# Attention with a mixture of experts on one core: six weight buffers, the first copies on ScalarE, later means, two steps run in the lead-in

## The chip, the cores and the metric

The kernel runs on one core of a Trainium2 chip. The metric is the device time of one execution in microseconds. Three runs of the kernel before gave a median of 1029.19 us (1027.43 to 1030.52). Five engines work side by side, each in the order of its own queue: TensorE (PE, matmuls and transposes), VectorE (DVE), ScalarE (ACT), GpSimd (POOL) and SyncE (SP), which here only issues DMAs.

## The reference

Four batches, eight heads, 576 positions, 64 features. Causal attention is mixed by a gate with a memory term, and the result goes through four experts whose outputs are summed with weights. All is fp32.

```python
scores = scale * np.matmul(q, k.transpose(0, 1, 3, 2))
scores = np.where(causal, -1000000000.0, scores)
a = np.exp(scores - scores.max(-1, keepdims=True))
a /= a.sum(-1, keepdims=True) + 1e-09
local = np.matmul(a, v)
q_p = phi(q)                       # elu(q) + 1
mem_out = einsum('bhsd,bhde->bhse', q_p, M_prev) / (einsum('bhsd,bhd->bhs', q_p, z_prev) + 1e-06)
x = g * mem_out + (1 - g) * local  # then [2304, 512]
p = domain_probs / (domain_probs.sum(-1, keepdims=True) + 1e-09)
for e in range(4):
    h = np.maximum(x @ w1[e], 0.0)       # [2304, 1024]
    out += p[:, e:e + 1] * (h @ w2[e])   # [2304, 512]
```

## The kernel before

Matmul operands are split into a high part (rounded) and a low part (what is left), and products are summed as high x high, high x low and low x high. So xh and xl, hh and hl, w1h and w1l, w2h and w2l, kha, khb and kl all are such parts.

The expert work runs in 40 phases. A phase is one half of one expert (four tiles of 128 hidden features, HF = 4) for one or two groups of 256 tokens: in phases 0 to 4 and 37 to 39 one group, between them two. In a phase the first layer makes h for the four tiles (`mm1`: matmuls L790, then hh on ScalarE L799 and hl on VectorE L800), then the second layer makes y (`mm2`: matmuls L820, accumulation on VectorE L834 and L836).

Each phase needs eight raw weight tiles of 256 KB. `w_dma` asks for a tile on SyncE's queue into a buffer of the tag stg; `w_prep` splits a tile (the high part on ScalarE, L205, or on GpSimd, L207; the low part mostly on GpSimd, L209) and then asks for the tile four further on. There were four buffers, so that tile went into the buffer just split.

The attention runs as 28 tasks of two heads each (12 of them joint, with the first 256 positions; 16 with the other 320) after a lead-in (`first_run`) that does the first 256 positions of batch 0 in an order written out by hand (the string ORDER; each word is a step). A task is cut into steps: load q, k, v (`t_load`), the feature map phi (ex on ScalarE, qp on VectorE L288, rl on GpSimd L292, rn on VectorE L300 to L310), transposes of q and k (`t_trq`, `t_trk`: tiles tq and tk), the split of v (`t_v`, L399 and L400), scores (`j_qk`, `s_qk`), exponentials, normalization, transposes of the probabilities (pt), the output (`j_o`, `s_o`). Scores are one matmul over 128 rows that hold the high part twice, so half of kha, khb and qz is copied to the other 64 partitions by DMAs from SBUF to SBUF (`dup_k` L352; the qz copies L371 and L376). Task i uses the set of buffers i % 2.

The memory matrices of a batch (mr) are split on GpSimd into ms (`batch_prep`, L231 and L232) once for each of the seven runs of four tasks; the output matmuls read ms.

Every step has a slot number and a priority within it. Sorted, they make one list, and a planner hands them out between the parts of the expert work, paced by estimated costs: a step is emitted when the share of attention done has fallen behind the share of expert work done (`target`). In the lead-in, words w1 and w3 also run the steps up to slots -9 and -8. What is emitted is each engine's order; nothing is reordered later.

Of the kernel before, what the change touches and what calls it, by code (L numbers as in the profile page):

```python
# [8 lines left out]
F32 = mybir.dt.float32  # L9
F32R = mybir.dt.float32r  # L10
# [39 lines left out]
def tile_attention_moe(  # L50
# [51 lines left out]
    sp = ctx.enter_context(tc.tile_pool(name="sp", bufs=2))  # L102
# [5 lines left out]
    def f(ap):  # L108
        return ap.bitcast(F32)
# [18 lines left out]
    for i in range(2):  # L128
        o, d = i * 13 * P, {}
# [39 lines left out]
    NSTG = 4  # L169
    wpos = {"dma": 0, "prep": 0}  # L170
    stg = {}

    def w_dma():
        j = wpos["dma"]
        if j >= len(wseq):
            return
        wpos["dma"] += 1
        i, kind, fc = wseq[j]
        e, hf = halves[i]
        f0 = (hf * HF + fc) * P  # L180
        t = sp.tile([P, DM], F32, tag="stg", name=f"stg{j}", bufs=NSTG)
        stg[j] = t
        if kind == "1":
            nc.sync.dma_start(
                out=t.rearrange("p (c f) -> p c f", c=NKD),
                in_=w1[e, :, f0 : f0 + P].rearrange("(c p) f -> p c f", p=P),
            )
        else:
            nc.sync.dma_start(out=t, in_=w2[e, f0 : f0 + P, :])
# [35 lines left out]

    def batch_prep(r):
        zb, mr, _ = bdat[r]
        ms = sp.tile([P, NPAIR, 4, D], F32R, tag="ms", name=f"ms{r[0]}_{r[1][0]}", bufs=2)
        m4 = mr.rearrange("p (a j) d -> p a j d", j=2)
        hi = ms[:, :, 0:4:3]  # L230
        nc.gpsimd.tensor_scalar(hi, m4, 1.0, 1.0, ALU.mult, ALU.mult)  # L231
        nc.gpsimd.tensor_tensor(ms[:, :, 1:3], m4, f(hi), ALU.subtract)  # L232
        bdat[r][2] = ms
# [7 lines left out]
    for b, cs in RUNS[1:]:  # L241
        for a in range(NPAIR):
            t = Task()
# [88 lines left out]
    def split_q(pt, qa, qb, n, scale):  # L332
        nc.scalar.activation(qa[A, 0:n], pt[A, 0:n], AF.Copy, scale=scale)
        nc.scalar.activation(qb[Bh, 0:n], pt[Bh, 0:n], AF.Copy, scale=scale)
        nc.vector.scalar_tensor_tensor(
            qa[Bh, 0:n], pt[A, 0:n], scale, f(qa[A, 0:n]), ALU.mult, ALU.subtract
        )
        nc.vector.scalar_tensor_tensor(
            qb[A, 0:n], pt[Bh, 0:n], scale, f(qb[Bh, 0:n]), ALU.mult, ALU.subtract
        )  # L340

    def split_k(pt, qk, c0, n):
        o = slice(c0, c0 + n)
        for x, k_ in ((A, qk["kha"]), (Bh, qk["khb"])):
            nc.scalar.activation(k_[x, o], pt[x, 0:n], AF.Copy)
        for x, k_ in ((A, qk["kha"]), (Bh, qk["khb"])):
            nc.vector.tensor_tensor(qk["kl"][x, o], pt[x, 0:n], f(k_[x, o]), ALU.subtract)

    def dup_k(qk, c0, n):
        o = slice(c0, c0 + n)  # L350
        for x, y, k_ in ((A, Bh, qk["kha"]), (Bh, A, qk["khb"])):
            nc.sync.dma_start(out=f(k_[y, o]), in_=f(k_[x, o]))  # L352

    def flat(ap):
        return ap.rearrange("p j d -> p (j d)")

    def t_trq(t):
        pt = to_tile(f"tq{t.i}")
        qk, last = t.qk, t.nk == NCH
        w = len(t.cs) * P  # L360
        for i in range(len(t.cs)):

            tr(pt[:, i * P : (i + 1) * P], flat(t.nat["q"][:, i]), P)
        if last:
            tr(pt[:, w : w + P], flat(t.nat["k"][:, 4]), P)
        split_q(pt, qk["qa"], qk["qb"], w, SCALE)
        if last:
            split_k(pt[:, w:], qk, 4 * P, D)
            dup_k(qk, 4 * P, D)
        for h, (x, q_) in enumerate(((A, qk["qa"]), (Bh, qk["qb"]))):  # L370
            nc.sync.dma_start(  # L371
                out=f(qk["qz"][x, h * GW : (h + 1) * GW]), in_=f(q_[x, 0:GW])
            )
            if last:
                o = 2 * GW + h * D
                nc.sync.dma_start(out=f(qk["qz"][x, o : o + D]), in_=f(q_[x, w - D : w]))  # L376

    def t_trk(t):
        pt = to_tile(f"tk{t.i}")
        m = min(t.nk, NCH - 1)  # L380
        for c in range(m):
            tr(pt[:, c * P : (c + 1) * P], flat(t.nat["k"][:, c]), P)
        split_k(pt, t.qk, 0, m * P)
        dup_k(t.qk, 0, m * P)

    def t_trqp(t):
        pt = to_tile(f"tp{t.i}")
# [296 lines left out]
    def ev(slot, prio, fn, cost=0.0):  # L684
        events.setdefault(slot, []).append((prio, len(events.get(slot, [])), fn, cost))

    seen = set()
    for t in tasks:
        s0 = t.s0
        ld = -9 + t.i if t.i < 2 else s0 - 7  # L690
        PQ = PR
        if t.run not in seen:
            seen.add(t.run)
            ev(s0 - (9 if t.i else 8), 9, lambda r=t.run: batch_load(r))
            ev(s0 + 1, 9, lambda r=t.run: batch_prep(r))
            if t.cs == CB and t.b == 0:
                for i in range(2):
                    ev(s0 - 12, 9, lambda i=i: zeros(i))
        ev(ld, 6.3 if t.cs == CA else 8, lambda t=t: t_load(t))
        ev(s0 + PQ["phi1"][0], PQ["phi1"][1], lambda t=t: t_phi1(t))  # L700
        ev(s0 + PQ["phi2"][0], PQ["phi2"][1], lambda t=t: t_phi2(t))
        ev(s0 + PQ["phi3"][0], PQ["phi3"][1], lambda t=t: t_phi3(t))
        if t.joint:
            ev(s0 - 3, 20, lambda t=t: t_phi4(t))
        ev(s0 + PQ["trq"][0], PQ["trq"][1], lambda t=t: t_trq(t), 109.0 * len(t.cs))
        ev(s0 + PQ["trk"][0], PQ["trk"][1], lambda t=t: t_trk(t), 109.0 * t.nk)
        ev(s0, PQ["v"], lambda t=t: t_v(t))
# [27 lines left out]
    steps = []  # L735
# [135 lines left out]
    def first_run():  # L871
# [201 lines left out]
        def f_w(j):  # L1073
            w_prep(0, "1" if j < HF else "2", True)
            if j in (1, 3):
                while si[0] < len(steps) and steps[si[0]][0] <= (-9 if j == 1 else -8):
                    run_step()

        def f_d(j):
            z_ = moe_bank(f"id{j}")  # L1080
            for _ in range(2):
                nc.tensor.matmul(z_, lhsT=hh[0][:, 0:P], rhs=hh[0], start=True, stop=True)
# [6 lines left out]
        rc4 sc5 nm20 pt2 rn0 sc7 m1 mk50 nm30 nm31 m0 sc6 mk51 pe2 pt3 nm40 nm41  # L1089
        ex50 ex51 tq0 w1 mk70 pe3 mk71 w2 rc5 eq0 tq1 eq1 w3 ex70 pt4 mk60 ou0 w4 d9  # L1090
        ex71 nm51 tq3 mk61 xh0 nm50 rc7 xl0 eq3 d2 ex61 nm71 pt5 ex60 rc6 nm70 pe4
        nm60 nm61 pe5 tq2 ou1 pt7 w5 eq2 pt6 pe7 xh1 ou2 xl1 pe6 w6 ou3 xh2 xl2 xh3
        xl3 w7 d12
        """
        calls = {k[2:]: g for k, g in locals().items() if k.startswith("f_")}

# [7 lines left out]
        for _ in range(NSTG):  # L1104
            w_dma()
        m4 = M_prev[b].rearrange("(a j) d e -> j d a e", j=2)
        for j in range(2):
            o = slice(j * D, (j + 1) * D)
# [10 lines left out]
        for word in ORDER.split():  # L1119
            name = word.rstrip("0123456789")  # L1120
# [8 lines left out]
        out=mask[:, 4 * P :],  # L1129
        in_=mask[:, 4 * P :],  # L1130
# [104 lines left out]
```

## Time and profile before

| | us |
|---|---|
| median of three runs | 1029.19 |
| profiled execution | 1027.72 |
| its span, first to last instruction | 1025.9 |
| busy in the span: TensorE | 1005.7 (98%) |
| VectorE | 671.5 (65%) |
| GpSimd | 581.4 (57%) |
| ScalarE | 487.3 (47%) |
| DMA queue of SyncE, share of 16 engines | 43.9% |

A busy time counts matmuls that may overlap at their ends, so a busy TensorE is not always TensorE at its peak. An idle time in brackets stands before an instruction, with what ended it. Names are the program's without buffer numbers; L and a number is a line of the kernel.

### The profile page before, as it was taken

Reading aid. Unit: us, or ns where it says so; the run is one execution under the profiler, and the core shown is the slowest. Engines: PE = TensorE matmul, PEld = TensorE weight load, DVE = VectorE, ACT = ScalarE, POOL = GpSimd, SP = SyncE. Lnnn points to the kernel's source line nnn. Section 1 sums busy time; section 2 is a strip of 40 time slices with the busy share of each in tenths; the row PEclk is TensorE's granted clock in tenths of the full one; section 3 lists DMA queues with packets and bytes.
Section 4 is the critical chain, followed back from the end, with each engine's and each line's share of the span. In section 5 each row is a group of like instructions: output and inputs, shape, how many; then the busy total and the mean of one; then the engine's idle time right before and its main releaser. Section 6 shows DMA issues by size and latency. Waiting matters only on the chain.

```text
span 1025.9 us, 16306 instructions
## 1 busy us (share of the span) xinstructions
PE 1005.7 (98%) x5202; PEld 844.8 (82%) x5202; DVE 671.5 (65%) x1662; ACT 487.3 (47%) x1156; POOL 581.4 (57%) x569
## 2 busy tenths in 40 slices
PE   8898999999999999999999999999999999999998
PEld 6787888887888888888888888888888888888887
DVE  6688878887778777877777777766665323222344
ACT  7576655654555545544454555544433213111243
POOL 6686857656555365546555455565553645656233
PEclk9999999999999999999999999999999999999999
DMA  6665564444535344445433544354331432433244
GB/s 150 160 175 163 142 164 112 139 126 116 132 101 128 110 128 111 114 127 135 103 100 109 146 123 118 91 144 111 86 98 54 132 93 82 130 97 101 74 137 141
DMA packets 213670, 123.17 MB, mean 120 GB/s; under 512 B 100688, under 2 KB 187728, under 8 KB 213584
## 3 DMA queue, kind: packets, MB, share of 16 engines
q1 hardware_dynamic: 213440, 122.12, 43.9%
q8 instruction: 42, 0.69, 0.3%
q14 instruction: 44, 0.36, 0.1%
q10 hardware_dynamic: 144, 0.00, 0.0%
HBM read 106.86 MB, written 4.72 MB: 109 GB/s over the span
## 4 chain that ended last, share of the span: by engine, by line
PE 86%; DVE 4%; POOL 3%; issue 3%; ACT 2%; DMA 1%; SPq 0%; POOLq 0%; DVEq 0%; ACTq 0%
PE y L820 36%; PE h L790 35%; PE sp L569 4%; PE pt L325 4%; PE o L670 4%; POOL w1l L209 1%; DVE rn L304 1%; PE tk L325 1%; POOL w2l L209 1%; PE tq L325 1%; PE tp L325 1%; ACT s L456 1%; DVE s L480 1%; PE sp L437 1%; DMA kha<-kha 1%
## 5 line engine op out<-in xcount | busy, mean ns | idle before, releaser
L209 POOL TENSOR_TENSOR w1l<-stg,w1h 128x512 fp32r<-128x512 f32 x152 | 198.3, 1316 | 312.2 <-ACT w1h L205 276.7
L790 PE MATMUL h<-xh,w1h 128*128 128x512 f32 (+1 forms) x640 | 247.9, 387 | 0.0
L790 PE MATMUL h<-xh,w1l 128*128 128x512 f32 (+1 forms) x640 | 237.5, 371 | 0.0
L820 PE MATMUL y<-w2h,hh 128*128 128x512 f32 x576 | 236.9, 411 | 0.0
L790 PE MATMUL h<-xl,w1h 128*128 128x512 f32 (+1 forms) x640 | 236.5, 370 | 0.0
L820 PE MATMUL y<-w2h,hl 128*128 128x512 f32 x576 | 227.1, 394 | 5.3 <-DVE hl L800 5.2
L820 PE MATMUL y<-w2l,hh 128*128 128x512 f32 x576 | 226.1, 393 | 0.9 <-POOL w2l L209 0.9
L209 POOL TENSOR_TENSOR w2l<-stg,w2h 128x512 fp32r<-128x512 f32 x152 | 199.2, 1313 | 43.4 <-ACT w2h L205 32.7
L799 ACT ACTIVATE hh<-h 128x512 fp32r<-128x512 f32 (+1 forms) x160 | 88.9, 556 | 252.5 <-PE h L790 251.4
L800 DVE SCALAR_TENSOR_TENSOR hl<-h,hh 128x512 fp32r<-128x512 f32 (+1 forms) x160 | 101.8, 636 | 131.7 <-ACT hh L799 130.7
L836 DVE SCALAR_TENSOR_TENSOR acc<-y,pn,acc 128x512 f32<-128x512 f32 x126 | 94.4, 749 | 73.7 <-PE y L820 72.1
L790 PEld LDWEIGHTS h<-xh,w1l 128*128 128x128 f32 x640 | 120.9, 189 | 21.6
L790 PEld LDWEIGHTS h<-xh,w1h 128*128 128x128 f32 x640 | 121.3, 190 | 16.3
L790 PEld LDWEIGHTS h<-xl,w1h 128*128 128x128 f32 x640 | 121.5, 190 | 15.6
L820 PEld LDWEIGHTS y<-w2h,hl 128*128 128x128 f32 x576 | 108.6, 189 | 31.0 <-DVE hl L800 7.1
L820 PEld LDWEIGHTS y<-w2l,hh 128*128 128x128 f32 x576 | 109.2, 190 | 18.8 <-POOL w2l L209 1.2
L820 PEld LDWEIGHTS y<-w2h,hh 128*128 128x128 f32 x576 | 109.0, 189 | 18.3 <-POOL w2h L207 0.2
L205 ACT ACTIVATE w1h<-stg 128x512 fp32r<-128x512 f32 x156 | 94.0, 625 | 12.0 <-DMA stg<-in_moe_w_dram 9.6
L612 ACT ACTIVATE pth<-pt 128x384 fp32r<-128x384 f32 (+3 forms) x128 | 50.5, 420 | 95.3 <-PE pt L325 94.9
L207 POOL TENSOR_SCALAR w2h<-stg 128x512 fp32r<-128x512 f32 x128 | 81.6, 638 | 15.7 <-PE y L820 15.7
L325 PE MATMUL pt<-ident,s 128*128 128x128 f32 (+1 forms) x376 | 60.7, 273 | 0.0
L577 DVE CUSTOM_DVE_ANT_0 s<-sp,mask 128x384 f32<-128x384 f32 (+1 forms) x96 | 53.0, 564 | 10.8 <-PE sp L569 10.1
(159 smaller groups left out, 1409.7 us busy)
## 6 DMA issues: line engine op xcount, KB each, us to landing
stg<-in_moe_w_dram SPq DMA_DIRECT2D x320, 256.0 KB, 2.9
natall<-in_k_dram SPq DMA_DIRECT2D x34, 128.0 KB, 2.7
out_dram<-acc SPq DMA_DIRECT2D x16, 256.0 KB, 2.1
natall<-in_v_dram SPq DMA_DIRECT2D x32, 128.0 KB, 2.6
natall<-in_q_dram SPq DMA_DIRECT2D x60, 64.0 KB, 2.8
kha<-kha SPq DMA_DIRECT2D x16, 128.0 KB, 2.8
khb<-khb SPq DMA_DIRECT2D x16, 128.0 KB, 2.4
natall<-in_k_dram SPq DMA_DIRECT2D x28, 64.0 KB, 2.4
```

What stands on the lines that cost most here:

```text
L205: nc.scalar.activation(hi, t, AF.Copy)
L207: nc.gpsimd.tensor_scalar(hi, t, 1.0, 1.0, ALU.mult, ALU.mult)
L209: (nc.vector if dve else nc.gpsimd).tensor_tensor(lo, t, f(hi), ALU.subtract)
L325: nc.tensor.transpose(dst, src, ident[0:n, 0:n])
L569: nc.tensor.matmul(pt[:, 0 : b_ - a], lhsT=q_, rhs=qk[k_][:, a:b_], start=y == 0, stop=y == len(pairs) - 1,)
L577: nc.vector.tensor_tensor_reduce(s.s[:, a:b_], pt[:, 0 : b_ - a], mask[:, m0 : m0 + b_ - a] if c < 4 else mask4[:, a:b_], 1.0, 3.0e38, ALU ...
L612: nc.scalar.activation(dh, src, AF.Copy)
L790: nc.tensor.matmul(pt[0][:, cols], lhsT=w_[:, c], rhs=x_[:, c, cols], start=(c == 0 and z == 0), stop=(c == NKD - 1 and z == 2),)
L799: nc.scalar.activation(h_, pt[0][:, cols], AF.Relu)
L800: nc.vector.scalar_tensor_tensor(l_, pt[0][:, cols], 0.0, f(h_), ALU.max, ALU.subtract)
L820: nc.tensor.matmul(pt[0], lhsT=h_[fc][:, tk], rhs=w_, start=(fc == 0 and z == 0), stop=(fc == HF - 1 and z == 2),)
L836: nc.vector.scalar_tensor_tensor(acc[g, tt], pt[0], pe, acc[g, tt], ALU.mult, ALU.add)
```

## The change

Five edits. The raw weights get six buffers instead of four; they are still asked for at the same places, four tiles ahead. The copies of task 0 to the other partitions are issued by ScalarE instead of SyncE; those of all later tasks stay. The means' split (ms) gets one buffer instead of two. It is prepared two slots after the start of a joint run (three slots, and first in its slot, for the others) instead of one. In the lead-in two new words, go5 and go4, run the steps up to slots -5 and -4.

```diff
-        t = sp.tile([P, DM], F32, tag="stg", name=f"stg{j}", bufs=NSTG)
+        t = sp.tile([P, DM], F32, tag="stg", name=f"stg{j}", bufs=NSTG + 2)
...
-        ms = sp.tile([P, NPAIR, 4, D], F32R, tag="ms", name=f"ms{r[0]}_{r[1][0]}", bufs=2)
+        ms = sp.tile([P, NPAIR, 4, D], F32R, tag="ms", name=f"ms{r[0]}_{r[1][0]}", bufs=1)
...
-    def dup_k(qk, c0, n):
+    def dup_k(qk, c0, n, eng):
         o = slice(c0, c0 + n)
         for x, y, k_ in ((A, Bh, qk["kha"]), (Bh, A, qk["khb"])):
-            nc.sync.dma_start(out=f(k_[y, o]), in_=f(k_[x, o]))
+            eng.dma_start(out=f(k_[y, o]), in_=f(k_[x, o]))
+
+    def copier(t):
+        return nc.sync if t.i else nc.scalar
...
         for h, (x, q_) in enumerate(((A, qk["qa"]), (Bh, qk["qb"]))):
-            nc.sync.dma_start(
+            copier(t).dma_start(
                 out=f(qk["qz"][x, h * GW : (h + 1) * GW]), in_=f(q_[x, 0:GW])
...
-            ev(s0 + 1, 9, lambda r=t.run: batch_prep(r))
+            ev(s0 + (2 if t.joint else 3), 9 if t.joint else 0.1, lambda r=t.run: batch_prep(r))
...
+        def f_go(j):
+            while si[0] < len(steps) and steps[si[0]][0] <= -j:
+                run_step()
...
-        nm60 nm61 pe5 tq2 ou1 pt7 w5 eq2 pt6 pe7 xh1 ou2 xl1 pe6 w6 ou3 xh2 xl2 xh3
-        xl3 w7 d12
+        nm60 nm61 pe5 tq2 ou1 pt7 w5 eq2 pt6 pe7 xh1 ou2 xl1 pe6 w6 ou3 go5 xh2 xl2
+        xh3 xl3 go4 w7 d12
```

ScalarE at the end of the lead-in, before the change (ex0 is phi of task 0, hh0 the first layer's first tile):

```order
L1001 ACTIVATE ptw6_539<-ptf6_524 128x256
L1066 ACTIVATE xh_95<-of2_530 128x256
L1066 ACTIVATE xh_95<-of3_545 128x256
L281 ACTIVATE ex0_564<-natall_73 128x256
L282 ACTIVATE ex0_564<-ex0_564 128x256
L345 ACTIVATE kha0_79<-tk0_578 64x256
L345 ACTIVATE khb0_80<-tk0_578 64x256
L799 ACTIVATE hh0_97<-h0_0_567 128x256
L333 ACTIVATE qa0_74<-tq0_604 64x256
L334 ACTIVATE qb0_75<-tq0_604 64x256
```

The same place after it:

```order
L1004 ACTIVATE ptw6_539<-ptf6_524 128x256
L281 ACTIVATE ex0_553<-natall_73 128x256
L282 ACTIVATE ex0_553<-ex0_553 128x256
L1069 ACTIVATE xh_95<-of2_530 128x256
L1069 ACTIVATE xh_95<-of3_545 128x256
L345 ACTIVATE kha0_79<-tk0_564 64x256
L345 ACTIVATE khb0_80<-tk0_564 64x256
L352 DMA kha0_79<-kha0_79 64x256
L352 DMA khb0_80<-khb0_80 64x256
L333 ACTIVATE qa0_74<-tq0_585 64x256
L334 ACTIVATE qb0_75<-tq0_585 64x256
L374 DMA qz0_76<-qa0_74 64x256
```

The feature map of task 0 moved ahead of two evictions, its k and q evictions ahead of the first hh, and the copies' issues stand between them (a second qz copy follows, then hh0).

GpSimd in phase 2, before (w1l is for this phase's first layer, w2l for its second; rl3 and v2 belong to attention tasks 3 and 2):

```order
L209 TENSOR_TENSOR w1l0_106<-stg16_828,w1h0_105 128x512
L209 TENSOR_TENSOR w1l1_108<-stg17_856,w1h1_107 128x512
L209 TENSOR_TENSOR w1l2_110<-stg18_884,w1h2_109 128x512
L209 TENSOR_TENSOR w1l3_112<-stg19_928,w1h3_111 128x512
L292 TENSOR_TENSOR rl3_1023<-qp3_1022,zb1_0_442 128x256
L399 TENSOR_SCALAR v2_1035<-natall_73 128x2x2x64
L400 TENSOR_TENSOR v2_1035<-natall_73,v2_1035 128x2x128
L209 TENSOR_TENSOR w2l0_114<-stg20_972,w2h0_113 128x512
```

The same place after:

```order
L209 TENSOR_TENSOR w1l0_106<-stg16_837,w1h0_105 128x512
L209 TENSOR_TENSOR w1l1_108<-stg17_865,w1h1_107 128x512
L292 TENSOR_TENSOR rl3_1011<-qp3_1010,zb1_0_442 128x256
L402 TENSOR_SCALAR v2_1019<-natall_73 128x2x2x64
L403 TENSOR_TENSOR v2_1019<-natall_73,v2_1019 128x2x128
L209 TENSOR_TENSOR w1l2_110<-stg18_909,w1h2_109 128x512
L209 TENSOR_TENSOR w1l3_112<-stg19_944,w1h3_111 128x512
L209 TENSOR_TENSOR w2l0_114<-stg20_979,w2h0_113 128x512
```

Three attention instructions moved ahead of two weight splits; phases 1 and 3 read alike.

VectorE in phase 2 before, from the gate pair (rn3 with gate) to the last hl:

```order
L304 TENSOR_SCALAR rn3_1109<-rn3_1109,gate_70 128x2 x2
L310 RECIPROCAL rn3_1109<-rn3_1109 128x4
L800 SCALAR_TENSOR_TENSOR hl2_103<-h2_2_1099,hh2_99 128x256
L470 TENSOR_SCALAR st8_1067<-st8_1067,ebp_69 128x1 x2
L478 RECIPROCAL st8_1067<-st8_1067 128x2
L480 TENSOR_SCALAR s8_1066<-s8_1066,st8_1067 128x128 x2
L335 SCALAR_TENSOR_TENSOR qa1_82<-tq3_1138,qa1_82 64x256
L338 SCALAR_TENSOR_TENSOR qb1_83<-tq3_1138,qb1_83 64x256
L800 SCALAR_TENSOR_TENSOR hl3_104<-h2_3_1134,hh3_100 128x256
L542 TENSOR_TENSOR xr_94<-o6_1162,otmp6_1173 64x256 x2
```

The same place after:

```order
L304 TENSOR_SCALAR rn3_1103<-rn3_1103,gate_70 128x2 x2
L310 RECIPROCAL rn3_1103<-rn3_1103 128x4
L473 TENSOR_SCALAR st8_1051<-st8_1051,ebp_69 128x1 x2
L481 RECIPROCAL st8_1051<-st8_1051 128x2
L483 TENSOR_SCALAR s8_1050<-s8_1050,st8_1051 128x128 x2
L335 SCALAR_TENSOR_TENSOR qa1_82<-tq3_1125,qa1_82 64x256
L338 SCALAR_TENSOR_TENSOR qb1_83<-tq3_1125,qb1_83 64x256
L803 SCALAR_TENSOR_TENSOR hl2_103<-h2_2_1099,hh2_99 128x256
L545 TENSOR_TENSOR xr_94<-o6_1147,otmp6_1158 64x256 x2
L803 SCALAR_TENSOR_TENSOR hl3_104<-h2_3_1143,hh3_100 128x256
```

hl2 moved behind the attention steps, and the xr pair in front of hl3.

## Rows read from the trace of the kernel before

**Rows 1.** Windows: us; busy PE, PEld, DVE, ACT, POOL; clock; DMA; GB/s.

```profile
25.00:50.00 25.00, 22.01 (x148) 18.98 (x147) 15.55 (x52) 13.92 (x42) 16.13 (x19) 0.93 0.63 158
50.00:75.00 25.00, 23.43 (x171) 21.56 (x170) 21.95 (x58) 19.59 (x53) 20.35 (x20) 1.00 0.64 174
75.00:100.00 25.00, 20.98 (x127) 17.46 (x126) 21.94 (x59) 16.16 (x43) 16.64 (x17) 0.96 0.61 168
...
225.00:250.00 25.00, 22.58 (x113) 18.96 (x113) 17.93 (x47) 12.27 (x30) 15.50 (x16) 0.93 0.46 118
250.00:275.00 25.00, 25.00 (x129) 20.90 (x128) 18.52 (x46) 13.21 (x32) 13.58 (x12) 1.00 0.40 103
```

**Rows 2.** Waits of TensorE: us in total, times, longest us.

```profile
PE y L820 <- DVE hl L800: 5.2, 3, 2.5
PE sp L437 <- DMA kha<-kha: 3.0, 1, 3.0
PE tk L325 <- DMA natall<-in_k_dram: 2.4, 1, 2.4
```

**Rows 3.** Timeline of SyncE near 31 us: start us, us, issue.

```profile
31.43 2.49 SPq L184 DMA_DIRECT2D stg<-in_moe_w_dram  x4
34.01 1.39 SPq L352 DMA_DIRECT2D kha<-kha  x1
```

**Rows 4.** Timeline of TensorE, ScalarE and VectorE around the first scores.

```profile
30.82 0.28 PE L790 MATMUL h<-xh,w1h 128*128 128x256 f32 x1
30.94 0.28 PE L790 MATMUL h<-xl,w1h 128*128 128x256 f32 x1
...
39.63 0.30 PE L437 MATMUL sp<-kha,qa 128*128 128x128 f32 x1 [2.99 <-DMA kha<-kha]
...
0.72 0.42 ACTq L1097 DMA_DIRECT2D betab<-in_beta_dram  x1
...
30.36 0.39 ACT L1066 ACTIVATE xh<-of 128x256 fp32r<-128x256 f32 x1 [1.32 <-PE of L1057]
...
30.78 0.42 DVE L1069 TENSOR_TENSOR xl<-of,xh 128x256 fp32r<-128x256 f32 x1 [1.28 <-ACT xh L1066]
```

**Rows 5.** DMA issues from 30 to 42 us; the last row, whole run.

```profile
kha<-kha SPq DMA_DIRECT2D x2, 64.0 KB, 4.1
...
qz<-qa SPq DMA_DIRECT2D x1, 64.0 KB, 3.7
...
qz<-qa SPq DMA_DIRECT2D x28, 64.0 KB, 2.0
```

**Rows 6.** Timeline of SyncE and TensorE near 238 us.

```profile
230.52 0.59 SPq L376 DMA_DIRECT2D qz<-qb  x1
231.22 4.16 SPq L189 DMA_DIRECT2D stg<-in_moe_w_dram  x3
...
237.11 1.14 SPq L263 DMA_DIRECT2D natall<-in_k_dram  x2
...
240.42 0.63 PE L325 MATMUL tk<-ident,natall 128*128 128x128 f32 x4 [2.42 <-DMA natall<-in_k_dram]
```

**Rows 7.** Timeline of VectorE, GpSimd and TensorE from 35 to 92 us.

```profile
35.02 0.36 DVE L304 TENSOR_SCALAR rn<-rn,gate 128x2 f32<-128x2 f32 x2
...
62.13 0.84 DVE L542 TENSOR_TENSOR xr<-o,otmp 64x256 f32<-64x256 f32 x2
...
89.98 2.38 DVE L304 TENSOR_SCALAR rn<-rn,gate 128x2 f32<-128x2 f32 x2
...
66.63 2.63 POOL L209 TENSOR_TENSOR w1l<-stg,w1h 128x512 fp32r<-128x512 f32 x2 [2.73 <-ACT w1h L205]
69.82 0.74 POOL L292 TENSOR_TENSOR rl<-qp,zb 128x256 f32<-128x256 f32 x1 [0.56 <-DVE qp L288]
...
71.72 5.08 POOL L209 TENSOR_TENSOR w2l<-stg,w2h 128x512 fp32r<-128x512 f32 x4
...
70.03 0.28 PE L790 MATMUL h<-xh,w1l 128*128 128x256 f32 x1
```

More of the change, by code (lines that the diff above doesn't have):

```diff
@@ L368, in t_trq @@
             split_k(pt[:, w:], qk, 4 * P, D)
-            dup_k(qk, 4 * P, D)
+            dup_k(qk, 4 * P, D, copier(t))
         for h, (x, q_) in enumerate(((A, qk["qa"]), (Bh, qk["qb"]))):
-            nc.sync.dma_start(
+            copier(t).dma_start(
                 out=f(qk["qz"][x, h * GW : (h + 1) * GW]), in_=f(q_[x, 0:GW])
@@ L383, in t_trk @@
         split_k(pt, t.qk, 0, m * P)
-        dup_k(t.qk, 0, m * P)
+        dup_k(t.qk, 0, m * P, copier(t))
     def t_trqp(t):
```

## The prediction

> **What bounds the kernel now.** I read the windows view first. TensorE is busy 25.00 of 25 us at a granted clock of 1.00 in 250 to 275 us [rows 1], and it stays so in every window up to 1000 us. Nothing can be won there by feeding it earlier, so the change is judged by the first 250 us and by whether it spoils the rest. The same view shows where something is lost: 25 to 50, 75 to 100 and 225 to 250 us are not full, and in them the clock is 0.93, 0.96 and 0.93. Since the clock has two levels (1.2 and 2.4 GHz), 0.93 over 25 us is 3.5 us at the lower level, which loses 25 x 0.07 = 1.75 us; 0.96 loses 1.0.
>
> Then the waits of TensorE [rows 2]. Three entries matter. The first scores wait 3.0 us once for a copy of kha. One transpose waits 2.4 us once for a load of k. Three second-layer matmuls wait 5.2 us in all for hl from VectorE, the longest 2.5. The clock belongs to these waits: the 3.0, the 2.5 and the 2.4 each lie in or just ahead of a window with a lowered clock, while 50 to 75 us, which holds one of the two shorter hl waits (2.7 together), kept 1.00 [rows 1, 2].
>
> **First copies (task 0).** Before, the four copies stand on SyncE's queue behind four weight loads: those take from 31.43 to 33.92, kha is issued at 34.01 and needs 1.39 us to issue, and the scores start at 39.63 after 2.99 us of idling [rows 3, 4]. Now ScalarE issues them. It finishes the last xh at 30.36 + 0.39 = 30.75; two key evictions of about 0.4 us (the order has them next) end near 31.6. An issue by ScalarE took 0.42 us [rows 4]; I take 0.5, so the k copies go out at 31.6 and 32.1, two q evictions follow, and the qz copies go out near 33.4 and 33.9.
>
> When TensorE asks for them: the transpose tq0 now stands ahead of the first layer and reuses the bank that the last xl frees at 30.78 + 0.42 = 31.2 [rows 4], so the first layer starts near 31.4 instead of 30.82 with two transposes inside it; that costs 0.3. In the order 27 short matmuls and one transpose lie between the first layer's start and the scores: 27 x 0.12 (their spacing in rows 4) + 0.15 = 3.4, so 34.8.
>
> When they land: from 30 to 42 us a copy of kha takes 4.1 us from issue to landing and one of qz 3.7; over the whole run a qz of this size takes 2.0 [rows 5]. With the busy stretch's numbers the last qz lands at 33.4 + 3.7 = 37.1, a wait of 2.3; with the quiet ones at 33.9 + 2.0 = 35.9, 1.1, and 0.6 if only the first qz is needed at once. I take 1.4, nearer the quiet end, because the copies no longer follow four loads in one queue, and no lowered clock, since it is close to the shorter hl waits. So 2.99 + 1.75 - 1.4 - 0.3 = 3.0 saved; ends 0.4 (wait 2.3 and the clock loss stays) and 3.8.
>
> A rule of the Trainium skill speaks against this term: DMA: Bandwidth & Descriptors, "Issuing engines are not separate DMA queues", says that DMAs of all issuing engines interleave on the same 16 DMA engines, so another issuer saves only issue time. By it the copies would still share with the four loads, and the sum would be by the lower end; that the copy of rows 5 took 4.1 in the busy stretch agrees with it.
>
> **Six weight buffers.** Loads are still asked for at the same places, four tiles ahead, but each goes into a buffer whose last reader is two tiles older, so SyncE need not wait for the tile just being split. Near 238 us this is the whole cause: the qz issues end at 230.52 + 0.59 = 231.1, then three weight loads take SyncE from 231.22 to 235.38, waiting for GpSimd's w1l, and the loads of q and k stand behind them, k at 237.11 [rows 6]. The order of SyncE is the same there after the change, with the same three weight loads between qz and the loads of q. At 0.5 to 0.6 each (an issue there takes 0.59) they would be done at 232.7 to 233.0 instead of 235.38, so k lands 2.4 to 2.7 us sooner. TensorE waited 2.42 for it, from 238.0 on. The wait goes, hardly to spare, and with it the clock loss: 2.42 + 1.75 = 4.2; I take 3.9. The ends are 0 (the buffer of k is freed late) and 4.2. Next late there would be the copies of that task's keys, for which TensorE waited only at the first task [rows 2]. ScalarE's waits for weights vanish too, worth nothing by themselves: ScalarE is not last there.
>
> **The order in phases 1 to 3 (about 50 to 100 us).** The steps that go5 and go4 run in the lead-in are off the list, so all later attention steps stand 9 to 12 short matmuls (1.1 to 1.4 us) further ahead in the expert work. Two queues pay for that. On GpSimd rl and v now stand ahead of w1l2 and w1l3. Before, this pair starts at 66.63 and takes 2.63, so the first ends at 67.9; TensorE reads it at 70.03, a margin of 2.1 [rows 7]. rl and v take from 69.82 to 71.72, 1.90, and rl cannot start before VectorE's qp. Were rl no earlier than now, w1l2 would end at 71.72 + 1.3 = 73.0, 3.0 late. But qp comes sooner, by those 1.1 us and by one accumulation that no longer precedes it (512 columns; from the 0.42 of 256 columns in rows 4 I count 0.7): 3.0 - 1.8 = 1.2 late. On VectorE hl2 and the xr pair now stand ahead of hl3 (0.84 for the pair [rows 7] and 0.42 for hl2, some 1.2 us more), and 9 more matmuls of 0.12 stand between on TensorE (1.1); so the hl wait stays, and partly falls inside the new one. VectorE's slow spot stays as well: the gate pair that takes 0.36 alone took 2.38 while GpSimd split w2 [rows 7]. Net per phase +1.2 - 0.7 = +0.5, three times 1.5; the lowered clock after the 2.5 us wait goes, -1.0. I take +0.5. The ends: all hl waits go with their clock loss, -6.2; or 3.0 more in each of three phases, +9.0, and a clock loss like the first copies' each time, +5.2 - 1.0.
>
> **Means in one buffer, later.** It is one GpSimd pass like w1l, 1.3 us, and a shorter one, some 1.9. It now waits for the previous run's last output matmuls, which precede it in the program anyway, and rl and the weight splits stand behind it. GpSimd idles more than that in most phases, so 0; ends -0.5 and +2. The shifts behind 250 us: 0, for TensorE never waits there [rows 1].
>
> **Sum.** -3.0 - 3.9 + 0.5 = -6.4. The profiled execution took 1027.72 us (its span 1025.9 and 1.8 around it), so 1021.3. It lies 1.5 below the median of 1029.19; on the median's footing 1022.8.
>
> **Rivals.**
> 1. The copies compete as before (the rule above): the first term gives 0.4. -0.4 - 3.9 + 0.5 = -3.8, 1025.4. For it: the 4.1 us copy in rows 5; against it: the copies go out 2.4 us earlier.
> 2. The first phases run smoothly: splitting starts sooner because weights are there, and the hl waits go. -3.0 - 3.9 - 6.2 = -13.1: 1016.1. Against it: the gate pair still meets GpSimd.
> 3. They eat the gain: a loss of about 2 in each of the three (between 0.5 and 3.0), +6 against the -6.9 of the first two terms, 1028.3.
> 4. Slower: in phases 1 to 3 TensorE waits for w1l2 on GpSimd, behind rl, which waits for VectorE. At 3.0 us and a lowered clock in each: -6.9 + 9.0 + 5.2 - 1.0 = +6.3, 1035.5. It decides from about 2.3 us a phase (6.9 / 3). For it: the margin of 2.1 against 1.90 of new work ahead; against it: the earlier qp.
> 5. The later load of k waits for something else as well and that term is lost: 1026.7.
>
> **How the numbers follow.** Forecast 0.47 (its own range 1019 to 1026), rival 1 0.13, rival 2 0.11, rival 3 0.12, rival 4 0.12, rival 5 0.05. A measurement of this kernel can tell about 0.3%, 3.1 us: faster is below 1026.1, slower above 1032.3. Faster: forecast, rivals 1 and 2, 0.71. Same: rivals 3 and 5, 0.17. Slower: 0.12. The range 1016 to 1029 leaves out most of rival 4 and half of rival 2.
>
> **What would show it.** The waits of TensorE for kha and for the load of k should be gone or under 1.5 us, and the clock 1.00 in 25 to 50 and 225 to 250 us; SyncE should no longer wait for w1l and w2l. The first copies should stand on ScalarE's queue near 31.6 us. A new wait of TensorE for w1l between 45 and 100 us decides the third term: above 2.3 us a phase I am wrong in sign. TensorE waiting anywhere past 260 us would make the last part wrong.

## The result and the profile after

The changed kernel took 1020.51 us, the median of six executions (1019.36 to 1023.09), beside 1029.45 for the kernel before on the same chip (six, 1027.23 to 1033.18). The ratio is 0.9914 with a 95% interval of 0.9891 to 0.9937: 8.9 us or 0.86% faster, 2.3 us below the forecast of 1022.8. The profiled execution of the changed kernel was the slowest of its six, 1023.09, so the two traces differ by 4.6 us only. The traces show where the time went; the medians say how much it is.

TensorE's waits in the changed kernel (columns: us in total, times, longest), which answer to [rows 2]:

```profile
PE h L793 <- POOL w1l L209: 3.5, 4, 2.0
PE y L823 <- DVE hl L803: 2.0, 1, 2.0
```

The load of k is gone from the list, the first scores wait 1.4 us in two pieces (below) instead of 3.0, hl has gone from 5.2 to 2.0, and a wait for w1l is new with 3.5. The windows that answer to [rows 1]:

```profile
25.00:50.00 25.00, 23.49 (x170) 19.89 (x169) 18.11 (x56) 16.75 (x50) 17.36 (x20) 1.00 0.71 180
50.00:75.00 25.00, 22.34 (x152) 20.76 (x152) 20.86 (x54) 17.47 (x48) 19.77 (x21) 0.93 0.65 169
75.00:100.00 25.00, 22.45 (x139) 18.68 (x138) 22.20 (x59) 16.61 (x45) 17.63 (x17) 1.00 0.61 172
...
225.00:250.00 25.00, 25.00 (x135) 21.16 (x134) 20.91 (x51) 13.87 (x33) 14.97 (x14) 1.00 0.49 134
```

The granted clock is back at 1.00 in 25 to 50 and 225 to 250 us, as forecast, and TensorE fills the latter window. A lowered clock of 0.93 has appeared in 50 to 75 us, where the kernel before had 1.00; 75 to 100 and 100 to 125 us, 0.96 and 0.97 before, have 1.00 now.

Where the time went is best read from a thing that both kernels do equally often: ScalarE's eviction hh, four in each of the 40 phases, 160 in every trace. The 33rd (the first of phase 8) and the 41st (phase 10), before and then changed:

```profile
206.40 0.60 ACT L799 ACTIVATE hh<-h 128x512 fp32r<-128x512 f32 x1 [0.48 <-PE h L790]
...
269.03 0.60 ACT L799 ACTIVATE hh<-h 128x512 fp32r<-128x512 f32 x1 [0.93 <-PE h L790]
```

```profile
205.54 0.60 ACT L802 ACTIVATE hh<-h 128x512 fp32r<-128x512 f32 x1 [0.48 <-PE h L793]
...
263.99 0.60 ACT L802 ACTIVATE hh<-h 128x512 fp32r<-128x512 f32 x1 [0.66 <-PE h L793]
```

The start of the 5th (first of phase 1), the stretches from there to these two and on to the last, and the start of the last:

| us | to phase 1 | phases 1 to 7 | 8 and 9 | 10 to the end | last hh |
|---|---|---|---|---|---|
| before | 52.0 | 154.4 | 62.6 | 747.6 | 1016.6 |
| changed | 50.1 | 155.4 | 58.5 | 748.0 | 1012.0 |
| difference | -1.9 | +1.0 | -4.1 | +0.4 | -4.6 |

The first copies fall in the first column, the order in phases 1 to 3 in the second, the load of k in the third. The first column holds more than the edits. ScalarE's last ptw, the last instruction of the lead-in ahead of those that moved, starts at 27.06 us before and at 28.34 in the changed kernel. Over the fourteen traces of this document it starts between 26.50 and 28.69, and no edit separates the early ones from the late (26.65 to 28.50 with four buffers, 26.50 to 28.69 with six). So up to 2.2 us of a difference in this column need not come from an edit.

**First copies.** ScalarE and TensorE in the changed kernel (start, duration, engine, line, instruction; idle time before it in brackets), beside [rows 3, 4]:

```profile
28.34 0.38 ACT L1004 ACTIVATE ptw<-ptf 128x256 f32<-128x256 f32 x1
...
32.42 0.52 ACTq L352 DMA_DIRECT2D kha<-kha  x1
...
34.08 0.47 ACTq L374 DMA_DIRECT2D qz<-qa  x1
```

```profile
36.68 0.30 PE L440 MATMUL sp<-kha,qa 128*128 128x128 f32 x1 [0.27 <-DMA kha<-kha]
...
38.12 0.19 PEld L440 LDWEIGHTS sp<-kl,qz 128*128 128x128 f32 x1 [1.28 <-DMA qz<-qa]
38.12 0.33 PE L440 MATMUL sp<-kl,qz 128*128 128x128 f32 x1 [1.14 <-DVE qp L288]
```

and what those copies took from issue to landing between 30 and 42 us, beside [rows 5]:

```profile
kha<-kha ACTq DMA_DIRECT2D x1, 64.0 KB, 4.1
...
qz<-qa ACTq DMA_DIRECT2D x1, 64.0 KB, 4.0
```

The copy of kha goes out at 32.42 instead of 34.01. It is no faster under way: 4.1 us, as before. The second wait is put down to VectorE's qp at the matmul, but at its weight load (PEld), of the same moment, to the first qz copy. That copy was issued at 34.08 and took 4.0, which gives 38.1, when the matmul starts; the copy is what it waited for.

**Load of k.** SyncE and TensorE in the changed kernel near 233 us, beside [rows 6]:

```profile
230.33 1.48 SPq L189 DMA_DIRECT2D stg<-in_moe_w_dram  x3
...
233.55 1.14 SPq L263 DMA_DIRECT2D natall<-in_k_dram  x2
```

```profile
236.94 0.60 PE L325 MATMUL tk<-ident,natall 128*128 128x128 f32 x4
```

The three weight loads hold SyncE for 1.5 us instead of 4.2, k goes out at 233.55 instead of 237.11, and the transpose waits for nothing. There is little to spare: the second of the two pieces of k was issued near 234.2 and took 2.6, which gives 236.8.

### The profile page after: what moved, and what is told of

The parts are those of the page before. It is cut to its first block, busy times and chain, and to the rows that moved or that the text cites. A ratio compares the mean times of both kernels' runs of the same rounds, so it can differ in the third digit from the quotient of the medians.

```text
span 1021.3 us, 16329 instructions
## 1 busy us (share of the span) xinstructions
PE 1004.2 (98%) x5202; PEld 843.9 (83%) x5202; DVE 677.1 (66%) x1662; ACT 485.5 (48%) x1156; POOL 581.5 (57%) x569
## 4 chain that ended last, share of the span: by engine, by line
PE 91%; DVE 4%; issue 2%; POOL 1%; ACT 1%; DMA 0%; POOLq 0%; DVEq 0%; ACTq 0%
PE y L823 37%; PE h L793 36%; PE sp L572 4%; PE pt L325 4%; PE o L673 4%; DVE rn L304 1%; PE tq L325 1%; PE tk L325 1%; PE tp L325 1%; PE id L1089 1%; PE sp L440 1%; DVE s L483 1%; PE o L520 1%; ACT s L459 1%; PE o L668 0%
## 5 line engine op out<-in xcount | busy, mean ns | idle before, releaser
L209 POOL TENSOR_TENSOR w2l<-stg,w2h 128x512 fp32r<-128x512 f32 x152 | 199.5, 1315 | 49.4 <-ACT w2h L205 36.8
```

The costliest lines, as they stand in the source:

```text
L209: (nc.vector if dve else nc.gpsimd).tensor_tensor(lo, t, f(hi), ALU.subtract)
```

## The experiments

All results in one table: the median, the ratio to runs of the kernel before on the same chip with its 95% interval, the profiled execution, the start of its last ptw, and its four stretches by hh as above.

| run | median us | ratio [interval] | profiled | last ptw | to phase 1 | 1 to 7 | 8, 9 | rest |
|---|---|---|---|---|---|---|---|---|
| e1_buffers | 1022.12 | 0.9936 [0.9913, 0.9959] | 1023.11 | 26.77 | 52.6 | 152.7 | 58.7 | 748.0 |
| e2_lead | 1023.52 | 0.9936 [0.9915, 0.9958] | 1023.68 | 26.65 | 49.4 | 153.3 | 62.4 | 747.5 |
| e3_copies_sync | 1024.65 | 0.9958 [0.994, 0.9975] | 1024.93 | 28.69 | 54.9 | 152.2 | 58.7 | 748.1 |
| e4_no_go | 1020.21 | 0.9907 [0.9876, 0.9939] | 1019.49 | 28.02 | 48.9 | 152.6 | 58.8 | 748.1 |
| e5_onlycopy | 1027.85 | 0.9989 [0.9975, 1.0003] | 1027.53 | 26.65 | 50.3 | 155.8 | 62.7 | 747.5 |
| e6_onlygo | 1028.54 | 1.0 [0.9979, 1.002] | 1031.84 | 28.50 | 56.6 | 153.5 | 62.9 | 747.5 |
| e7_four | 1025.6 | 0.9972 [0.996, 0.9984] | 1025.37 | 27.02 | 51.4 | 153.4 | 61.9 | 747.5 |
| e8_late_w | 1018.97 | 0.9907 [0.9889, 0.9925] | 1018.95 | 26.97 | 48.7 | 152.7 | 58.4 | 748.0 |
| e9_means1 | 1019.68 | 0.9905 [0.9875, 0.9935] | 1017.3 | 26.90 | 49.1 | 150.4 | 58.7 | 748.0 |
| e10_late_go | 1018.31 | 0.9893 [0.9867, 0.9918] | 1017.67 | 26.50 | 47.9 | 151.4 | 59.2 | 748.1 |
| e11_late_m1 | 1018.16 | 0.9893 [0.9862, 0.9925] | 1018.34 | 28.05 | 49.4 | 151.2 | 58.5 | 748.0 |
| e12_all | 1018.68 | 0.9896 [0.9869, 0.9923] | 1020.83 | 28.64 | 50.5 | 152.6 | 58.6 | 748.0 |

### Six buffers and later means alone (e1_buffers)

The kernel before with:

```
-... name=f"stg{j}", bufs=NSTG)
+... name=f"stg{j}", bufs=NSTG + 2)
-... name=f"ms{r[0]}_{r[1][0]}", bufs=2)
+... name=f"ms{r[0]}_{r[1][0]}", bufs=1)
-ev(s0 + 1, 9, ... batch_prep(r))
+ev(s0 + (2 if t.joint else 3), 9 if t.joint else 0.1, ... batch_prep(r))
```

> Only the six weight buffers and the later means in one buffer; copies on SyncE and the lead-in as before. Theory A (three separate terms): the wait of TensorE for the load of k near 238 us goes with its lowered clock, about -4 us; the first scores still wait about 3 us for kha with a lowered clock, because the four copies still stand behind four weight loads; the waits for hl in 50 to 125 us stay near 6 us. So 1029.5 - 4 = 1025.5, 0.996 of before. Rival B (early weights drive the first phases): ScalarE no longer waits for weights, the hl waits shrink too, and this alone gives nearly all of the gain, 1021 to 1022.

Measured 1022.12, 0.1 above the range of rival B and well below the 1025.5 of theory A. Phases 8 and 9 take 58.7 instead of 62.6: the wait for k is gone. The first scores still wait 2.7 us for the copies, with a clock of 0.86 in 25 to 50 us. In phases 1 to 7 it also gained 1.7 in its profiled execution: the hl waits fell from 5.2 to 3.0, the longest from 2.5 to 1.5. This run moved the means as well, but e11, with six buffers and the first means at the old place, has the same 3.0, and e5, with four buffers, has 5.1. That speaks for the buffers: they helped the first phases too, which the forecast had not counted.

### Copies on ScalarE and the lead-in words alone (e2_lead)

The changed kernel with:

```
-... name=f"stg{j}", bufs=NSTG + 2)
+... name=f"stg{j}", bufs=NSTG)
-... name=f"ms{r[0]}_{r[1][0]}", bufs=1)
+... name=f"ms{r[0]}_{r[1][0]}", bufs=2)
-ev(s0 + (2 if t.joint else 3), 9 if t.joint else 0.1, ... batch_prep(r))
+ev(s0 + 1, 9, ... batch_prep(r))
```

> Only the copies of task 0 on ScalarE and the two lead-in steps; four weight buffers and the means as before. Theory A: the first scores wait 1 to 2 us instead of 3 and the clock stays up, -3; the wait for the load of k near 238 us stays at about 2.4 us with its lowered clock; about 3 us of waits for w1l appear in phases 1 to 4 and some of the hl waits go. So 1026 to 1027. Rival B: no gain, 1029.

Measured 1023.52, a larger gain than either theory gave, though its eight executions spread from 1020.33 to 1026.17. Phases 8 and 9 stay at 62.4, the k wait with them (2.2 us); phase 1 starts at 49.4, 2.6 earlier than before (0.4 of it by the earlier ptw), and the clock of 25 to 50 us is 1.00.

### The changed kernel with the copies back on SyncE (e3_copies_sync)

```
     def copier(t):
-        return nc.sync if t.i else nc.scalar
+        return nc.sync
```

> The changed kernel with task 0's copies back on SyncE. Theory A: the copies stand behind four weight loads (issued up to 37.5 us in the changed kernel's profile), so TensorE waits for kha or qz 4 us or more and its clock drops; 3 to 6 us slower than the changed kernel, 1024 to 1026. Rival (the rule that another issuer saves only issue time): under 1 us slower, 1021 to 1021.5.

Measured 1024.65, 4.1 above the changed kernel, with intervals that don't overlap: theory A. SyncE and the first scores in this run:

```profile
32.72 1.86 SPq L184 DMA_DIRECT2D stg<-in_moe_w_dram  x3
34.67 0.53 SPq L352 DMA_DIRECT2D kha<-kha  x1
...
36.57 0.47 SPq L374 DMA_DIRECT2D qz<-qa  x1
```

```profile
39.96 0.30 PE L440 MATMUL sp<-kha,qa 128*128 128x128 f32 x1 [3.19 <-DMA kha<-kha]
41.46 0.33 PE L440 MATMUL sp<-kl,qz 128*128 128x128 f32 x1 [1.21 <-DMA qz<-qa]
```

The copies stand behind three weight loads, and qz behind a fourth. Counted from the last ptw, the first qz is issued 2.1 us later than in the changed kernel and takes 4.9 instead of 4.0. So what the other queue is worth is mostly this place in the line.

### The changed kernel without the lead-in words (e4_no_go)

```
-  ... ou3 go5 xh2 xl2 xh3 xl3 go4 w7 d12
+  ... ou3 xh2 xl2 xh3 xl3 w7 d12
```

> The changed kernel without the two lead-in steps: copies on ScalarE, six buffers, late means. Theory A: the waits for w1l in phases 1 to 4 (3.5 us in the changed kernel) disappear, the waits for hl come back to 5 us or so; the first scores wait 1 to 2 us. Together within 2 us of the changed kernel, 1019 to 1023. Rival (the lead-in steps are what makes the copies early enough): the scores wait 3 us again with a lowered clock, 1025.

Measured 1020.21, which can't be told from the changed kernel: theory A. The w1l waits fall from 3.5 to 0.4 us, the hl waits rise from 2.0 to 3.0 (three, longest 1.5), and the clock is 1.00 in every window up to 275 us. With six buffers and later means in place the words change which engine is waited for, not the time as far as these medians can tell.

### The copies alone (e5_onlycopy)

The kernel before with:

```
-            nc.sync.dma_start(out=f(k_[y, o]), in_=f(k_[x, o]))
+            eng.dma_start(out=f(k_[y, o]), in_=f(k_[x, o]))
... (the qz copies likewise; eng is ScalarE for task 0, else SyncE)
```

> Before with one edit: the four copies of task 0 issued by ScalarE. Theory A (each term by itself): only the first scores' wait changes, from 3.0 us to between 0.7 and 1.4, and the clock of 25 to 50 us is 1.00; the 2.4 us wait for natall and the hl waits between 50 and 100 us stay as before. Against a before of 1028.8 that is 1025.5 to 1027. Rival B (the places of the steps in phases 1 to 3 decide more than the terms): the hl waits shrink as well although nothing there was edited, and the time falls to 1023 to 1024.5, as far as the copies and the two lead-in words did together.

Measured 1027.85, a gain of 0.5 whose interval reaches 1: neither theory. The window and the wait in this run:

```profile
25.00:50.00 25.00, 23.10 (x160) 20.19 (x158) 17.11 (x57) 14.86 (x44) 17.50 (x21) 0.93 0.69 165
```

```profile
38.22 0.33 PE L440 MATMUL sp<-kl,qz 128*128 128x128 f32 x1 [1.90 <-DMA qz<-qa]
```

The wait only fell to 1.9 and the lowered clock stayed; of the 1.7 us gained up to phase 1 (0.4 of it by the earlier ptw), 1.3 went again in phases 1 to 7, where an hl wait of 2.3 and a clock of 0.93 in 75 to 125 us stand.

### The lead-in words alone (e6_onlygo)

The kernel before with:

```
-  ... ou3 xh2 xl2 xh3 xl3 w7 d12
+  ... ou3 go5 xh2 xl2 xh3 xl3 go4 w7 d12
```

> Before with one edit: the words go5 and go4 in the lead-in. Theory A (the forecast's third term): w1l waits of about 1 us come in and hl waits shrink by as much; the first copies still wait 3 us for kha, natall still 2.4; 1028 to 1030. Rival B: the earlier steps alone take the lowered clock and most hl waits away, 1025 to 1027. Rival C: the w1l waits cost more than the hl waits gave, over 1031.

Measured 1028.54, no change: theory A. Its profiled execution was 3.3 us above its median; its last ptw is 1.4 later than before. In it the first scores wait 3.9 and 1.2 us, and the clock of 25 to 50 us is 0.86: with the copies on SyncE, asking for them earlier only made TensorE wait longer.

### The changed kernel with four buffers (e7_four)

```
-... name=f"stg{j}", bufs=NSTG + 2)
+... name=f"stg{j}", bufs=NSTG)
```

> The changed kernel with four weight buffers instead of six, all else kept. Theory A: the wait of about 2.4 us for natall near 238 us returns with a clock of 0.93 in 225 to 250 us, 4 us more than the changed kernel: 1023.5 to 1025.5; and since the means are worth nothing, it equals the kernel with the copies and the two words alone (1023.5) within 1 us. Rival B (the buffers are not why that load came sooner, the order is): no such wait, 1020 to 1021.5. If the means' buffer costs something, it shows as over 1025.5.

Measured 1025.6, 5.1 above the changed kernel: the wait returns, theory A, at a time 0.1 above its range. SyncE, ScalarE and TensorE in this run, and the two larger pieces of k (when they were issued, and how long they took to land):

```profile
229.54 4.14 SPq L189 DMA_DIRECT2D stg<-in_moe_w_dram  x3
```

```profile
237.45 0.52 ACT L281 ACTIVATE ex<-natall 128x384 f32<-128x384 f32 x1 [5.51 <-DMA natall<-in_q_dram]
...
238.44 0.58 ACT L802 ACTIVATE hh<-h 128x512 fp32r<-128x512 f32 x1
```

```profile
239.08 0.63 PE L325 MATMUL tk<-ident,natall 128*128 128x128 f32 x4 [2.78 <-ACT hh L802]
```

```profile
L263 SPq DMA_DIRECT2D natall<-in_k_dram x2: 505/550/594, 235.4 to 236.1; - x2
...
DMA to landing us min/median/max: 2.9/3.1/3.2
```

The profile names hh, which ends at 239.02. But in the changed kernel the same transposes start at 236.94 while that hh (236.81, 0.58 us) is still running, so they don't wait for it. The second piece of k, issued at 236.1, took 2.9 and landed at 239.0: the load of k is the wait here too. The load of q, ahead of it behind the weight loads, is late as well, and ScalarE's queue stands 5.5 us on it (3.1 in the changed kernel); that this costs TensorE anything is not shown. The clock stayed at 1.00 in this window (phases 8 and 9 took 61.9 instead of 62.6), so the lowered clock need not follow such a wait. And the time is 2.1 above e2_lead, from which this kernel differs by the means alone; I had expected them equal within 1. By the traces that difference lies ahead of phase 1 (51.4 against 49.4), where the clock of 25 to 50 us is 0.93 here and 1.00 in e2. Phases 1 to 7 take 153.4 and 153.3: a w1l wait of 1.9 here, an hl wait of 2.1 in e2, each with a window at 0.93. Why the stretch ahead of phase 1 differs stays open.

### Weight loads held back behind the copies (e8_late_w)

The changed kernel without go5 and go4, and with:

```
+    hold = [False, 0]
+
     def w_dma():
+        if hold[0]:
+            hold[1] += 1
+            return
...
         def f_w(j):
+            if j == HF:
+                hold[0] = True
...
         dup_k(t.qk, 0, m * P, copier(t))
+        if t.i == 1:
+            hold[0] = False
+            for _ in range(hold[1]):
+                w_dma()
```

> The changed kernel without go5 and go4 (1020.2), and the four weight loads that are issued while task 0's copies are under way (1 MB from 31.3 us) asked for only behind the key copies of task 1 (about 39 us). Theory A (the copies are slow because they share the DMA engines with those loads): kha, khb and the two qz copies land in 2.5 us or less instead of 2.7 to 4.0, the scores no longer wait for qz (0.7 before), 1018.5 to 1020. Rival B (a copy of this kind takes that long by itself or because of the other loads from 26 to 31 us): landing stays at 2.7 to 4.0, the time stays within 0.5 of 1020.2. Rival C: phase 1 waits for its weights, which come 8 us later, over 1022.

The same four copies in this run:

```profile
kha<-kha ACTq DMA_DIRECT2D x1, 64.0 KB, 1.9
...
qz<-qb ACTq DMA_DIRECT2D x1, 64.0 KB, 2.0
```

All four land in 1.9 to 2.0 us, beside 2.7 to 4.0 in e4, from which this kernel differs by the hold alone, and the scores wait for nothing: theory A. Of the time little is gained, since a later load of k, now behind the held loads, makes a transpose wait 0.6: 1018.97 against 1020.21, the profiled executions differ by 0.5, and the intervals overlap.

### The first means at their old place (e9_means1)

The changed kernel with, for the first run of tasks alone:

```
-ev(s0 + (2 if t.joint else 3), ...
+ev(s0 + (1 if not t.i else 2 if t.joint else 3), ...
```

> The changed kernel with the means of the first run of tasks (batch 0) prepared one slot after its start, as before, instead of three; all other runs later as changed. On GpSimd the two ms instructions then stand ahead of phase 1's w1l0 instead of between w1l1 and rl. Theory A (the w1l wait of 2.0 us near 53 us comes from those 1.9 us of GpSimd work, so the later means cost what the forecast put at nothing): that wait goes or falls under 0.6, the clock of 50 to 75 us returns to 1.00, and the time falls by 2 to 3.5 us to 1017 to 1018.5. Rival B (the two lead-in words alone set that wait): it stays within 0.5 of 2.0 and the time at 1020 to 1021. Rival C (another hl wait takes its place): w1l wait gone, hl waits of 1.5 to 2.5 in 50 to 80 us, 1019 to 1020.5.

GpSimd in the changed kernel and the matmul that waits:

```profile
45.77 2.57 POOL L209 TENSOR_TENSOR w1l<-stg,w1h 128x512 fp32r<-128x512 f32 x2 [3.48 <-ACT w1h L205]
48.31 0.62 POOL L231 TENSOR_SCALAR ms<-mr 128x512 fp32r<-128x512 f32 x1
49.01 1.29 POOL L232 TENSOR_TENSOR ms<-mr,ms 128x512 fp32r<-128x512 f32 x1
...
52.75 2.53 POOL L209 TENSOR_TENSOR w1l<-stg,w1h 128x512 fp32r<-128x512 f32 x2
```

```profile
54.07 0.39 PE L793 MATMUL h<-xh,w1l 128*128 128x256 f32 x1 [1.97 <-POOL w1l L209]
```

and in this run, with ms moved ahead:

```profile
44.24 2.56 POOL L209 TENSOR_TENSOR w1l<-stg,w1h 128x512 fp32r<-128x512 f32 x2 [2.38 <-ACT w1h L205]
48.04 0.74 POOL L292 TENSOR_TENSOR rl<-qp,zb 128x256 f32<-128x256 f32 x1 [1.24 <-DVE qp L288]
...
49.93 2.56 POOL L209 TENSOR_TENSOR w1l<-stg,w1h 128x512 fp32r<-128x512 f32 x2
```

```profile
PE h L797 <- POOL w1l L209: 1.1, 3, 0.4
```

VectorE's pair ahead of qp, in the changed kernel and in this run:

```profile
48.55 1.90 DVE L483 TENSOR_SCALAR s<-s,st 128x256 f32<-128x256 f32 x2
```

```profile
47.01 0.62 DVE L483 TENSOR_SCALAR s<-s,st 128x256 f32<-128x256 f32 x2
```

The ms work of 1.9 us stood between w1l1 and w1l2, and with it gone the longest w1l wait is 0.4: theory A on the cause. From the end of w1l1 to w1l2 it is 3.1 us instead of 4.4. The ms work costs 1.3 there and not 1.9, for without it GpSimd idles 1.24 for VectorE's qp; with it qp comes later too, since the pair ahead of qp takes 1.90 while ms runs and 0.62 here, and rl waits for it 0.56 behind ms. The wait needs the words as well: in e4 and e1, with the later means but without the words, w1l2 and w1l3 stand ahead of ms, and the w1l waits are 0.4 in all. The profiled execution, 1017.3, is where A put the time. It is the fastest of its four, with a ptw 1.4 earlier than the changed kernel's and an hl wait of 0.3 where that one has 2.0 (the last section), so it is no measure of this edit. The median, 1019.68 (1017.3 to 1021.29), lies where rival C put it, and can't be told from the changed kernel's; that other executions have C's hl wait is not shown.

### Both findings (e10_late_go, e11_late_m1, e12_all)

e10 is the changed kernel with the loads held back, e11 is e8 with the first means at the old place, e12 is the changed kernel with both edits.

> The changed kernel whole, with the four weight loads held back behind task 1's key copies. Theory A (the lead-in words pay only by sending the copies out earlier, and that is worth nothing once they land in 2 us): no wait of the first scores beyond 0.6, but the w1l wait of 2 us and the lowered clock at 50 to 75 us as in the changed kernel: 1019.5 to 1021, about 1 to 1.5 slower than without the words (1018.97). Rival B: the words still gain, under 1018.5.

> The changed kernel without go5 and go4, with the four weight loads held back, and the first run's means prepared at the old place. Theory A (the means cost something only where w1l is late, and without the words it is not): 1018.5 to 1019.5, no change from 1018.97. Rival B: the hl waits of 1.7 and 1.4 us at 58 and 75 us move as well, under 1018 or over 1020.

> The changed kernel whole, with both findings: the four weight loads held back behind task 1's key copies, and the first run's means prepared at the old place. Theory A (the two add up: the qz wait of 1.0 to 1.3 us goes through the late loads, the w1l wait of 2.0 us at 53 us through the means' place): clock 1.00 in every window up to 125 us, no TensorE wait over 1.5 us behind 30 us, 1016 to 1017.5, below each of the two alone (1018.3 and 1019.7). Rival B (each repair uncovers the same next wait): no wait over 1.5 us either, but 1018 to 1019. Rival C (holding the loads back makes phase 1's w1l late once the means no longer hide it): a w1l wait over 1 us near 50 us, over 1018.5.

They measured 1018.31, 1018.16 and 1018.68. e10 has rival B's time, but 0.7 under e8 is less than its own spread (1017.4 to 1019.01); its w1l wait was 1.1, not 2, and its clock 1.00 from 50 to 75 us, so theory A's second half failed. Its kha and khb, issued at 30.58 and 31.20 (in e8 at 32.27 and 32.89), took 3.5 and 3.1, its qz 2.2 and 2.0: the four loads that were held are not the only ones that slow a copy. e11's time lies between its theories; its hl waits stayed at 3.0 in all, as in e8, which speaks for A. e12 did not add the two up: rival B's time, though its profiled execution, with a late ptw, has a wait of 2.0 (below). These three and e8 lie 1.5 to 2.4 us under the changed kernel, with intervals that overlap its; all are faster than before, and none is shown to be better than the changed kernel or another.

## Why the prediction was right

**First copies, -3.0: right in size, partly by luck, and not a term by itself.** The last ptw is 1.28 late in the changed kernel's trace, and still phase 1 starts 1.9 earlier, so the stretch saved 3.1. The first layer starts 32.73 - 30.82 = 1.9 later, 0.6 of it beyond that lead-in, where I took 0.3. The wait left is 1.4, as taken, but not for the reason given. I put the landing nearer the quiet 2.0; kha took 4.1 and the first qz 4.0, above my busy 3.7. Less the 1.28, that qz went out at 32.8 instead of 33.4, and TensorE asked for the scores at 35.1 instead of 34.8; these two made up for the landing. That is luck. The rule of the Trainium skill that I weighed (DMA: Bandwidth & Descriptors, "Issuing engines are not separate DMA queues") has the DMAs of all issuers interleave on the same 16 DMA engines. The landing agrees: 3.6 to 4.1 us on ScalarE's queue too, and 1.9 to 2.0 in e8, without the loads beside them. By that rule the other issuer saves issue time alone, which is usually small. Here the other issuer was worth 4.1 us (e3), because on SyncE the copies stand behind the loads' issues. What I missed is that this term needs its neighbours: e5 alone gained 0.5; with the lead-in words, which send kha out at 30.73 instead of 31.96 from the same ptw, e2 gained 5. With six buffers e4 lies 1.9 below e1, within the intervals of both.

**Six buffers, -3.9: right.** -4.1 in the trace and -3.9 in e1's; e7 gives 5.1 back by the medians, 3.4 of it in phases 8 and 9 by the traces. One sign failed: SyncE still waits for the weights:

```profile
SPq L189 <- POOL w1l L209: 258.2, 107, 12.1
SPq L184 <- POOL w2l L209: 178.4, 97, 5.6
```

in the kernel before, and in the changed one

```profile
SPq L352 <- ACT khb L345: 185.5, 24, 12.3
SPq L189 <- POOL w1l L209: 93.2, 43, 12.1
...
SPq L184 <- POOL w2l L209: 52.6, 29, 4.1
SPq L184 <- POOL w1l L209: 38.3, 27, 4.5
SPq L189 <- POOL w2l L209: 29.2, 22, 1.6
```

About half of that wait is left, 213 us instead of 437, and SyncE now waits to issue copies (khb) instead; the buffers removed the waits that TensorE saw, not all.

**Order in phases 1 to 3, +0.5: right in sum, wrong in its parts.** Measured +1.0 over phases 1 to 7. The first of the four w1l waits took 2.0, with a clock of 0.93 in its window; the other three took 1.5 together, below the 1.2 a phase that I worked out. That first one came from the means together with the words (e9, e4); the means I put at 0 because GpSimd idles more than 1.9 us in most phases. It does, but not at that place: ms stands ahead of a w1l that TensorE is about to read. So the means are the term that was mis-sized. In this trace the wait is worth 2.0 and the window's clock 25 x 0.07 = 1.75; by the medians nothing of it is clear, for moving the means back (e9) gained 0.8, inside the noise, and 2.1 of e7 against e2 lies elsewhere. The hl waits fell by 3.2, more than the 2.1 counted, partly, it seems, through the buffers (e1). And the clock that I gave back there, 1.0, left out 100 to 125 us: 0.97 before, 1.00 now, 1.75 with the other.

**Past 250 us, 0: right in size, but a sign against it came up.** From phase 10 to the end it is +0.4: every trace with six buffers has 748.0 to 748.1 there, every one with four 747.5 to 747.6. And TensorE waits once past 260 us, for a matmul that reads qpb and ms:

```profile
652.45 0.38 PE L668 MATMUL o<-qpb,ms 128*128 128x320 f32 x1 [0.39 <-DVE qpb L338]
```

All ten traces in which the later runs' means come later have this wait of 0.4, and the other four have none; so the later means cost something there, if little.

**The rest of the gain.** The forecast's sum was -6.4, the traces differ by 4.6, the medians by 8.9. The profiled execution of the changed kernel, the slowest of its six, has two things that other executions need not have: the ptw late by 1.28, and the hl wait of 2.0 that the last section follows. That its other five executions were free of them would fit their times; no trace of them shows it, so this stays open, and that the median came within 2.3 of the forecast is no proof of the sum.

## What to carry to other kernels

A transfer that the critical path needs should not stand in a queue behind bulk loads, nor move beside them: here the place in the queue was worth 4.1 us, and beside the loads a copy took up to twice as long to land (e8). Before an edit is costed at nothing because an engine idles elsewhere, look at what stands right behind it in that engine's order and who reads that next. Terms of one stretch don't add up: measure an edit beside its neighbours as well as alone.

## What the runs showed of the hardware

Two tiny VectorE instructions can take microseconds beside GpSimd. The gate pair (128x2) takes 0.36 us alone [rows 7]. In the changed kernel and in e9 it starts just after GpSimd begins three w2l in a row:

```profile
88.36 3.86 POOL L209 TENSOR_TENSOR w2l<-stg,w2h 128x512 fp32r<-128x512 f32 x3
```

```profile
88.44 3.80 DVE L304 TENSOR_SCALAR rn<-rn,gate 128x2 f32<-128x2 f32 x2
```

(changed), and in e9

```profile
84.34 3.82 POOL L209 TENSOR_TENSOR w2l<-stg,w2h 128x512 fp32r<-128x512 f32 x3
```

```profile
84.42 2.51 DVE L304 TENSOR_SCALAR rn<-rn,gate 128x2 f32<-128x2 f32 x2
```

In one it ends with the third w2l, in the other with the second: same order, same start, 1.3 us apart. Where it is the longer one, TensorE waits 2.0 for hl, until 95.83; e12's profiled execution, the slowest of its six (1015.61 to 1020.83), has it again:

```profile
85.46 3.79 DVE L309 TENSOR_SCALAR rn<-rn,gate 128x2 f32<-128x2 f32 x2
```

with a clock of 0.93 in its window, while e8, where that pair takes 1.68, ran four times within 0.1 us. The Trainium skill has an exclusive lock on a port pair that VectorE and GpSimd share (SBUF — State Buffer, "Who interferes with whom"); that the pair ends only when a GpSimd instruction ends agrees. So does the pair at L483 shown under e9: 1.90 us in the changed kernel, ending when ms does (50.45 and 50.30), and 0.62 where no ms runs beside it.

The lowered clock is no fixed price of a wait: 2.42 for k was followed by 0.93 before [rows 1, 2], 2.78 in e7 by 1.00, and the hl wait of 2.0 at 95 us in the changed kernel by 1.00, the same wait in e12 by 0.93. The 2.7 for kha in e1 was followed by 0.86, twice the loss. So my 1.75 a wait fits the waits for kha and for k in the kernel before, and would have been wrong for others.
